# Local and global attention with a gated feed-forward: global rows of batches 4 to 7 loaded, cast and transposed later, and the last q and k of batch 1 ahead of the last w_in columns

## The chip, the core and the metric

The kernel runs on one core of one Trainium2 chip. The metric is the device time of one execution in microseconds (us). A core has TensorE (PE, matmuls; PEld is its weight load), VectorE (DVE), ScalarE (ACT), GpSimd (POOL) and SyncE (SP); here SP issues nearly all DMAs, and POOL a few. Each engine takes its instructions in the order of its own queue and waits on semaphores for others.

## The reference

Eight batches, eight heads, 512 local and 32 global rows of width 64. A global row attends to all 544 rows, a local row to the 32 global ones and to the local ones within 32 places. Then the heads are put side by side (512 columns) and go through a feed-forward with 2048 hidden columns.

```python
k_all = np.concatenate([k_g, k_l], axis=2); v_all = np.concatenate([v_g, v_l], axis=2)
out_g = np.matmul(sm(scale * np.matmul(q_g, k_all.transpose(0, 1, 3, 2))), v_all)
mask = np.abs(pos[:, None] - pos[None, :]) <= 32
s_ll = np.where(mask, scale * np.matmul(q_l, k_l.transpose(0, 1, 3, 2)), -1e9)
s_lg = scale * np.matmul(q_l, k_g.transpose(0, 1, 3, 2))
out_l = np.matmul(sm(np.concatenate([s_lg, s_ll], axis=-1)), v_all)
x = np.concatenate([out_g, out_l], axis=2).transpose(0, 2, 1, 3).reshape(-1, 512)
h = x @ w_in
out = (h * np.clip(h + 3.0, 0.0, 6.0) / 6.0) @ w_out
```

## The kernel before

**Pairs and batches.** The unit of attention is a pair of heads: pair p is batch b = p // 4 with m = p % 4, so there are 32 pairs. Pairs 0 to 7 (batches 0 and 1) stand in a sequence written out by hand; pairs 8 to 31 run in one loop (L760). Between the parts of a pair, `M(n)` puts n units of the feed-forward of an earlier batch. A unit of the first kind (`u1`, L421) makes 128 hidden columns from `win`: 4 matmuls into `psH`, then ACT (L426) and DVE (L428) make `gt`. One of the second kind (`u2`, L437) adds 4 matmuls to an output tile `po`. PSUM tiles come from one pool of 7 banks.

**One pair.** `load(p)` (L121, L124): SP loads k, q and v into three of 16 staging tiles `stg`. `cast(p)` (L137): POOL makes fp16 of them; `vshift` (L141) copies v once more, shifted by half a block, into `vb`. For pairs 0 to 7 `emit_T(p)` (L223) transposes k and q on TensorE; later pairs use DMA transposes issued by SP, `emit_TD(p)` (L244 for kT, L245 for qT), and a short POOL copy, `wrap_q(p)` (L251). `emit_S2(p)` (L263) makes the scores in two halves of 8 matmuls, each ending in ACT's exponential (L267) and a mask on DVE (L270). In tile `kT`, which holds all four pairs of a batch, each block is 128 local columns and 32 global ones; the first half of the scores reads local columns alone, the second also the global ones. `emit_SG(p)` (L306) scores the global rows; `emit_AV(p)` (L332, L335) and `emit_PG(p)` multiply by v; `emit_X(p)` sends the result `xn` back by a DMA transpose of SP (L388), or, for batches 0 and 1 and pair 11, by TensorE (L393).

**Global rows.** k_g and q_g come in three steps: `load_g(b0, b1, name)` (SP, L180), `cast_G` (POOL or DVE, L188), `emit_G` (4 TensorE transposes into `psGT`, L198, then 4 DVE copies into `kgT` or `qgz`, L206). For batches 4 to 7 each name is one load, one cast and one `emit_G`. `kglob(b)` (POOL, L210) copies kgT of batch b into the global columns of that batch's kT tile; kT tiles alternate between two.

**Order.** Within the loop everything for SP and POOL is put in the program's order by `pin`. At the top of pair p stands `feed(p)` (L708), with work for later pairs: `wrap_q(p + 2)`; at m = 0 two POOL copies of the next batch's v_g (L144, L149); `cast(p + 4)` and `vshift(p + 4)`; `kglob(b + 1)` at m = 1; then on SP `emit_TD(p + 3)` and `load(p + 5)`. After it come the scores of pair p + 1, `emit_SG(p + 1)`, `emit_AV(p)`, `emit_PG(p)` and `emit_X(p)`, with units between. The global rows of batches 4 to 7 are loaded at p = 9, cast on POOL at p = 11 and transposed at p = 12.

**The beginning.** The loads stand in one list. Each load of w_in (L160) is 512 columns of one of four row blocks, so that columns 1536 to 2047, units 12 to 15, need loads 12 to 15. POOL casts (L171) most of them in the same order as they are loaded.

Of the kernel before, what the change touches and what calls it, by code (L numbers as in the profile page):

```python
# [14 lines left out]
def kernel(  # L15
# [12 lines left out]
    nc = tc.nc  # L28
    P = 128
    B, H, Sl, D = q_l.shape  # L30
# [3 lines left out]
    NM = H // 2  # L34
# [20 lines left out]
    def ps_tile(name, dtype=FP32):  # L55
        return psp.tile([P, 2048 // (4 if dtype == FP32 else 2)], dtype, tag="ps", name=name)
# [54 lines left out]
    def stage():  # L111
        return wrk.tile([P, 512], FP32, tag="stg", name="stg", bufs=NSTG)

    def load(p, what="kqv"):
        b, m = divmod(p, NM)
        s = st.setdefault(p, {})
        for c in what:
            src = {"k": k_l, "q": q_l, "v": v_l}[c]
            t = stage()
            if c != "v" and b < NRUN:  # L120
                nc.sync.dma_start(out=t.rearrange("p (h x) -> p h x", h=2),  # L121
                                  in_=src[b, 2 * m:2 * m + 2].rearrange("h (p j) d -> p h (j d)", j=NT))
            else:
                nc.sync.dma_start(out=t.rearrange("p (h kb d) -> p (h kb) d", h=2, kb=NT),  # L124
                                  in_=src[b, 2 * m:2 * m + 2].rearrange("h (kb p) d -> p (h kb) d", p=P))
            s[c + "f"] = t.rearrange("p (h kb d) -> p kb h d", h=2, kb=NT)

    def cast(p, what, eng):
        b, m = divmod(p, NM)
        s = st[p]  # L130
        for c in what:
            if c == "v":
                o = vts[b % NV][:, :, m, vc].rearrange("p kb (h d) -> p kb h d", h=2)
            else:
                s[c + "n"] = wrk.tile([P, NT, P], FP16, tag=c + "n", name=c + "n", bufs=4)
                o = s[c + "n"].rearrange("p kb (h d) -> p kb h d", h=2)
            eng.tensor_copy(out=o, in_=s[c + "f"])  # L137

    def vshift(p, eng):
        b, m = divmod(p, NM)  # L140
        eng.tensor_copy(out=vbs[b % NV][0:D, :, m, vc], in_=vts[b % NV][D:P, :, m, vc])  # L141

    def vglob(b, eng):
        eng.tensor_copy(out=vbs[b % NV][rg, :, :, vc],  # L144
                        in_=vg[rg, b].rearrange("s (m h) d -> s m (h d)", h=2).unsqueeze(1)
                        .to_broadcast([Sg, NT, NM, P]))

    def vgsum(b, eng):
        eng.tensor_copy(out=vgs[b % NV][rg], in_=vg[rg, b])  # L149

    def load_vg(b):
        nc.gpsimd.dma_start(out=vg[rg, b], in_=v_g[b].rearrange("h s d -> s h d"))
# [3 lines left out]
    def load_w(kind, i):  # L156
        t = stage()
        if kind == "in":
            qd, m = divmod(i, NM)
            nc.sync.dma_start(out=t, in_=moe_w_in[m * P:(m + 1) * P, qd * 512:(qd + 1) * 512])  # L160
        else:
            nc.sync.dma_start(out=t, in_=moe_w_out[i * P:(i + 1) * P, :])
        w_st[kind, i] = t

    def cast_w(kind, i, eng):
        if kind == "in":
            qd, m = divmod(i, NM)
            o = w_in_t[m][:, qd * 512:(qd + 1) * 512]
        else:
            o = w_out_t[i // 4][:, i % 4]  # L170
        (eng.copy if eng is nc.scalar else eng.tensor_copy)(out=o, in_=w_st[kind, i])  # L171
# [5 lines left out]
    def load_g(b0, b1, nm):  # L177
        src = {"kg": k_g, "qg": q_g}[nm]
        t = stage()
        nc.sync.dma_start(  # L180
            out=t[:, 0:(b1 - b0) * HH * D].rearrange("p (n d) -> p n d", d=D),
            in_=src[b0:b1].rearrange("b (x y) s d -> (y s) (b x) d", x=HH))
        gst[b0, nm] = t

    def cast_G(b0, b1, nm, eng=nc.vector):
        n = wrk.tile([P, 4 * P], FP16, tag="gn", name=nm + "n", bufs=2)
        nb = b1 - b0
        eng.tensor_copy(out=n[:, 0:nb * P], in_=gst[b0, nm][:, 0:nb * P])  # L188
        gst[b0, nm, "n"] = n

    def emit_G(b0, b1, nm):
        nb = b1 - b0
        if (b0, nm, "n") not in gst:
            cast_G(b0, b1, nm)
        n = gst[b0, nm, "n"]
        psT = ps_tile("psGT", FP16)
        for j in range(nb):
            nc.tensor.matmul(out=psT[:, j * P:(j + 1) * P], lhsT=n[:, j * P:(j + 1) * P],  # L198
                             rhs=ident, is_transpose=True)
        MH = NM // HH  # L200
        for x in range(HH):
            kv = psT[x * D:(x + 1) * D, 0:nb * P].rearrange("p (b m e s) -> p e b m s", b=nb, m=MH, e=2)
            for e in range(2):
                r, ms = slice(e * D, (e + 1) * D), slice(x * MH, (x + 1) * MH)
                o = kgT[r, ms, b0:b1] if nm == "kg" else qgz[r, ms, b0:b1, e]
                nc.vector.tensor_copy(out=o.rearrange("p m b s -> p b m s"), in_=kv[:, e])  # L206

    def kglob(b, eng):
        kv = kTs[b % 2][:, :, 0:NT * KW].rearrange("p m (u c) -> p m u c", u=NT)
        eng.tensor_copy(out=kv[:, :, :, P:KW],  # L210
                        in_=kgT[:, :, b].unsqueeze(2).to_broadcast([P, NM, NT, Sg]))
# [37 lines left out]
    def wrap_q(p):  # L249
        qT = st[p]["qT"]  # L250
        nc.gpsimd.tensor_copy(out=qT[:, 0:W], in_=qT[:, Sl:Sl + W])  # L251
# [130 lines left out]
    def emit_X(p):  # L382
        b, m = divmod(p, NM)
        xn = st[p]["xn"]
        if b > NRUN or (b == NRUN and m < NM - 1):
            xt = wrk.tile([P, Sl], FP16, tag=f"xt{m}", name=f"xt{m}", bufs=2)
            xts.setdefault(b, []).append(xt)
            nc.sync.dma_start_transpose(out=xt.rearrange("p (w c) -> p w c", w=NT),  # L388
                                        in_=xn.rearrange("p w c -> p (w c)"))
            return  # L390
        psX = ps_tile("psX", FP16)
        for w in range(NT):
            nc.tensor.matmul(out=psX[:, w * P:(w + 1) * P], lhsT=xn[:, w], rhs=ident,  # L393
                             is_transpose=True)
        xt = wrk.tile([P, Sl], FP16, tag=f"xt{m}", name=f"xt{m}", bufs=2)
        xts.setdefault(b, []).append(xt)
        nc.vector.tensor_copy(out=xt, in_=psX[:, 0:Sl])  # L397
# [68 lines left out]
    def M(n):  # L466
        for _ in range(n):
            if units:
                units.pop(0)()
# [26 lines left out]
    load(6, "kq")  # L496
    load(4, "v")
    load(5, "v")
    for i in range(12, NC):
        load_w("in", i)  # L500
    load(7, "kq")
    load(6, "v")
    load(7, "v")
    load_g(0, 4, "qg")
# [58 lines left out]
    def first(p, what="kqv"):  # L563
        cast(p, what, nc.gpsimd)
        vshift(p, nc.gpsimd)
# [15 lines left out]
    cast(6, "kq", nc.gpsimd)  # L581
    first(4, "v")
    first(5, "v")
    for i in range(12, NC):
        cast_w("in", i, nc.gpsimd)
    cast(7, "kq", nc.gpsimd)
    first(6, "v")
    first(7, "v")
    vgsum(0, nc.gpsimd)
# [118 lines left out]
    def feed(p):  # L708
        b, m = divmod(p, NM)
        if 2 * NM <= p + 2 < NPAIR:  # L710
            wrap_q(p + 2)
        if p + 4 < NPAIR:
            if m == 0:
                vglob(b + 1, nc.gpsimd)
                vgsum(b + 1, nc.gpsimd)
            cast(p + 4, "kqv", nc.gpsimd)
            vshift(p + 4, nc.gpsimd)
        if m == 1 and b + 1 < B:
            kglob(b + 1, nc.gpsimd)
        if m == 2 and b + 2 < B:  # L720
            load_vg(b + 2)
        if 2 * NM <= p + 3 < NPAIR:
            emit_TD(p + 3)
        if p + 5 < NPAIR:
            load(p + 5)
# [34 lines left out]
    for p in range(2 * NM, NPAIR):  # L760
        b, m = divmod(p, NM)
        feed(p)
        if p == 9:
            load_g(4, B, "kg")
            load_g(4, B, "qg")
        if p == 11:
            cast_G(4, B, "kg", nc.gpsimd)
            cast_G(4, B, "qg", nc.gpsimd)
        if p == 12:
            emit_G(4, B, "kg")  # L770
            emit_G(4, B, "qg")
        n = (1, 1, 1, 2) if p == 2 * NM else (1, 1, 2, 2) if b == 2 else (1, 2, 2, 3)
        M(n[0])
        if m == 0 and b > NRUN:
            emit_den(b - 1)
            emit_XG(b - 1)
        if p + 1 < NPAIR:
            emit_S2(p + 1)
        M(n[1])
        if p + 1 < NPAIR:  # L780
            emit_SG(p + 1)
        M(n[2])
        emit_AV(p)
        emit_PG(p)
        M(n[3])
        emit_X(p)
        if m == NM - 1:
            units += moe_units(lambda mm, b=b: xts[b][mm], Sl, local_dests(b), last=(b == B - 1))
        pin(*QUEUES)
# [41 lines left out]
```

## Time and profile before

| | |
|---|---|
| Median of 13 runs | 328.85 us (327.89 to 330.01) |
| The profiled execution | 329.3 us |
| Its span, first to last instruction | 327.5 us |
| Mean granted TensorE clock | 0.979 |
| DMA | 53.57 MB, mean 164 GB/s |

The page cuts the span into 40 slices of 8.19 us; a digit is the busy share in tenths:

```profile
PE   7898789999994899999999999999999999999995
...
DVE  6758639799662669747974697469755882379201
ACT  6758736888450369636973697369736970479100
POOL 4866697598873865474567445845331110000000
...
DMA  8999989999999997988878998978744003100132
```

And the chain of work that ended last, by engine:

```profile
PE 81%; DMA 7%; DVE 3%; SPq 3%; POOL 2%; ACT 2%; issue 1%; POOLq 0%
```

In the busy rows, a low digit of PE is a stretch in which TensorE waited, or in which little was to be done (the start and the end). In a timeline each row is start, length, engine, line, operation and tiles; brackets give the idle time of the engine before it and what ended that. "SPq" rows are SP's issuing of DMAs. All times are from the span's start.

### The profile page before, as it was taken

What the parts mean: (1) busy time and instruction counts of PE and PEld (TensorE: products, weight loads), DVE (VectorE), ACT (ScalarE), POOL (GpSimd) and SP (SyncE); (2) the same over time, 40 slices, a digit from 0 to 9 for tenths busy, and PEclk for the clock granted to TensorE, in tenths of its full rate; (3) what the DMA queues carried; (4) which work ended last, traced back from release to release, by engine and by line L of the source; (5) the groups of instructions that cost most, each with busy time, mean ns of one, the idle gap of its engine ahead of it and who ended that gap; (6) DMA issues with size and microseconds to landing.
All of it is one profiled execution on the core that took longest, in us unless ns stands there. A gap on an engine that the chain in (4) does not pass through costs nothing.

```text
span 327.5 us, 7295 instructions
## 1 busy us (share of the span) xinstructions
PE 309.2 (94%) x2657; PEld 162.8 (50%) x2657; DVE 212.8 (65%) x480; ACT 198.3 (61%) x396; POOL 157.0 (48%) x295
## 2 busy tenths in 40 slices
PE   7898789999994899999999999999999999999995
PEld 4454346554552455555555555555555554448444
DVE  6758639799662669747974697469755882379201
ACT  6758736888450369636973697369736970479100
POOL 4866697598873865474567445845331110000000
PEclk9999959999999599999999999999999999999999
DMA  8999989999999997988878998978744003100132
GB/s 205 250 286 321 242 237 330 233 183 219 189 218 203 187 213 146 148 193 202 164 147 197 212 148 151 206 197 151 142 118 110 16 16 92 70 0 2 32 90 73
DMA packets 142436, 53.57 MB, mean 164 GB/s; under 512 B 129728, under 2 KB 134080, under 8 KB 142400
## 3 DMA queue, kind: packets, MB, share of 16 engines
q1 hardware_dynamic: 140224, 52.84, 70.9%
q0 software_dynamic: 2176, 0.26, 2.0%
q8 instruction: 21, 0.34, 0.5%
q14 instruction: 15, 0.12, 0.2%
HBM read 35.13 MB, written 8.91 MB: 134 GB/s over the span
## 4 chain that ended last, share of the span: by engine, by line
PE 81%; DMA 7%; DVE 3%; SPq 3%; POOL 2%; ACT 2%; issue 1%; POOLq 0%
PE po L437 35%; PE psH L421 32%; PE psS L263 4%; DMA stg<-in_v_l_dram 3%; DMA stg<-in_moe_w_in_dram 2%; DMA stg<-in_q_l_dram 2%; PE pav L332 2%; PE pav L335 2%; DVE gt L428 2%; SPq L121 2%; PE psSG L306 1%; PE pg L372 1%; PE po L449 1%; PE psS L276 1%; ACT t L426 1%
## 5 line engine op out<-in xcount | busy, mean ns | idle before, releaser
L437 PE MATMUL po<-wout,gt 128*128 128x512 f16 x528 | 124.2, 383 | 0.0
L421 PE MATMUL psH<-xt,win 128*128 128x512 f16 x512 | 120.4, 381 | 0.5 <-DVE xt L397 0.5
L428 DVE SCALAR_TENSOR_TENSOR gt<-t,psH 128x512 f16<-128x512 f32 (+1 forms) x144 | 90.9, 652 | 30.4 <-ACT t L426 29.1
L426 ACT ACTIVATE t<-psH,half_col 128x512 f32<-128x512 f32 (+1 forms) x144 | 92.0, 669 | 16.7 <-PE psH L421 15.5
L421 PEld LDWEIGHTS <-win 128*128 128x128 f16 x576 | 53.3, 98 | 52.4 <-issue 1.2
L437 PEld LDWEIGHTS <-gt 128*128 128x128 f16 x528 | 48.9, 99 | 53.4 <-issue 1.0
L267 ACT ACTIVATE E<-psS 128x512 f16<-128x512 f32 x96 | 49.4, 604 | 17.2 <-PE psS L263 17.1
L270 DVE TENSOR_TENSOR E<-E,mk 128x512 f16<-128x512 f16 x96 | 50.8, 565 | 11.6 <-ACT E L267 10.5
L441 ACT COPY ot<-po 128x512 f32<-128x512 f32 x16 | 9.4, 587 | 45.7 <-PE po L437 45.2
L137 POOL CAST kn<-stg 128x512 f16<-128x512 f32 x31 | 19.3, 623 | 27.4 <-DMA stg<-in_k_l_dram 27.0
L358 POOL TENSOR_TENSOR s<-Eg 128x128 f32<-128x128 f16 x24 | 11.3, 471 | 43.2 <-ACT Eg L307 42.9
L340 DVE TENSOR_TENSOR xn<-pav,rc 128x256 f16<-128x256 f32 x64 | 26.1, 422 | 1.4
L441 DVE COPY ot<-po 128x512 f32<-128x512 f32 x17 | 11.7, 689 | 21.1 <-PE po L437 17.4
L137 POOL CAST qn<-stg 128x512 f16<-128x512 f32 x31 | 19.3, 621 | 12.8 <-DMA stg<-in_q_l_dram 12.2
L137 POOL CAST vt<-stg 128x512 f16<-128x512 f32 x32 | 20.1, 627 | 8.6 <-DMA stg<-in_v_l_dram 7.8
L141 POOL COPY vb<-vt 64x512 f16<-64x512 f16 x32 | 20.5, 639 | 2.1
L292 ACT ACTIVATE E<-psS 128x512 f16<-128x512 f32 x32 | 17.3, 598 | 5.2 <-PE psS L288 4.9
L332 PE MATMUL pav<-vt,E 128*128 128x65 f16 x256 | 20.4, 195 | 0.0
L335 PE MATMUL pav<-vb,E 128*128 128x65 f16 x256 | 20.4, 196 | 0.0
L332 PEld LDWEIGHTS <-E 128*128 128x128 f16 x256 | 18.2, 100 | 3.5 <-issue 0.2
L335 PEld LDWEIGHTS <-E 128*128 128x128 f16 x256 | 17.2, 98 | 3.0
L405 ACT ACTIVATE Lg<-pg 64x128 f32<-64x128 f32 x16 | 4.3, 269 | 22.5 <-PE pg L379 22.4
(93 smaller groups left out, 284.3 us busy)
## 6 DMA issues: line engine op xcount, KB each, us to landing
stg<-in_k_l_dram SPq DMA_DIRECT2D x32, 256.0 KB, 3.5
stg<-in_q_l_dram SPq DMA_DIRECT2D x32, 256.0 KB, 4.4
stg<-in_v_l_dram SPq DMA_DIRECT2D x32, 256.0 KB, 4.8
out_dram<-ot SPq DMA_DIRECT2D x23, 256.0 KB, 3.3
stg<-in_moe_w_in_dram SPq DMA_DIRECT2D x16, 256.0 KB, 6.1
stg<-in_moe_w_out_dram SPq DMA_DIRECT2D x16, 256.0 KB, 4.7
out_dram<-ot SPq DMA_DIRECT2D x8, 192.0 KB, 3.9
out_dram<-ot SPq DMA_DIRECT2D x16, 64.0 KB, 1.9
```

The costliest lines, as they stand in the source:

```text
L137: eng.tensor_copy(out=o, in_=s[c + "f"])
L141: eng.tensor_copy(out=vbs[b % NV][0:D, :, m, vc], in_=vts[b % NV][D:P, :, m, vc])
L267: nc.scalar.activation(out=E[:, ch, e], in_=pss[2 * ch + e], func=EXP, scale=qk_scale)
L270: nc.vector.tensor_tensor(out=E[:, ch, e], in0=E[:, ch, e], in1=mk[:, ch].rearrange("p w c -> p (w c)"), op=mult)
L332: nc.tensor.matmul(out=o, lhsT=E[:, 0, e, w * P:(w + 1) * P], rhs=vt[:, w, m, c], start=True, stop=False, skip_group_check=True)
L335: nc.tensor.matmul(out=o, lhsT=E[:, 1, e, w * P:(w + 1) * P], rhs=vb[:, (w - 1) % NT, m, c], start=False, stop=True, skip_group_check=True)
L340: nc.vector.tensor_tensor(out=xn[:, 2 * w2:2 * w2 + 2].rearrange("p w (e d) -> p w e d", e=2), in0=po[:, :, 1:1 + P].rearrange("p w (e d) ...
L421: nc.tensor.matmul(out=ps[:, 0:n], lhsT=w_in_t[m][:, c * P:(c + 1) * P], rhs=rhs(m), start=(m == 0), stop=(m == NM - 1), skip_group_check= ...
L426: nc.scalar.activation(out=t1[:, 0:n], in_=ps[:, 0:n], func=RELU, bias=half_col, scale=1.0 / 6.0)
L428: nc.vector.scalar_tensor_tensor(out=gts[c][:, 0:n], in0=t1[:, 0:n], scalar=1.0, in1=ps[:, 0:n], op0=amin, op1=mult)
L437: nc.tensor.matmul(out=po[t][:, 0:dm], lhsT=gts[c][:, t * P:(t + 1) * P], rhs=w_out_t[c // 4][:, c % 4], start=(c == 0), stop=(c == NC - 1))
L441: (nc.scalar.copy if t % 2 else nc.vector.tensor_copy)(out=ot, in_=po[t][:, 0:dm])
```

## The change

Three edits. The load and the cast of k and q of pair 7 stand ahead of loads and casts 12 to 15 of w_in. The global rows of batches 4 to 7 are loaded at p = 10 instead of 9, cast at p = 12 instead of 11, and transposed at p = 14 instead of 12, the q rows at the end of that pair, ahead of `emit_X`. And `kglob(4)`, which reads what the transpose of the k rows makes, moves from pair 13 (m = 1) to pair 15 (m = 3), in both cases behind the casts in `feed`; the other batches keep m = 1. No instruction is added or taken away.

```diff
@@ -496,9 +496,9 @@
     load(6, "kq")
     load(4, "v")
     load(5, "v")
+    load(7, "kq")
     for i in range(12, NC):
         load_w("in", i)
-    load(7, "kq")
     load(6, "v")
     load(7, "v")
     load_g(0, 4, "qg")
@@ -581,9 +581,9 @@
     cast(6, "kq", nc.gpsimd)
     first(4, "v")
     first(5, "v")
+    cast(7, "kq", nc.gpsimd)
     for i in range(12, NC):
         cast_w("in", i, nc.gpsimd)
-    cast(7, "kq", nc.gpsimd)
     first(6, "v")
     first(7, "v")
     vgsum(0, nc.gpsimd)
@@ -715,7 +715,7 @@
                 vgsum(b + 1, nc.gpsimd)
             cast(p + 4, "kqv", nc.gpsimd)
             vshift(p + 4, nc.gpsimd)
-        if m == 1 and b + 1 < B:
+        if m == (NM - 1 if b == 3 else 1) and b + 1 < B:
             kglob(b + 1, nc.gpsimd)
         if m == 2 and b + 2 < B:
             load_vg(b + 2)
@@ -760,15 +760,14 @@
     for p in range(2 * NM, NPAIR):
         b, m = divmod(p, NM)
         feed(p)
-        if p == 9:
+        if p == 10:
             load_g(4, B, "kg")
             load_g(4, B, "qg")
-        if p == 11:
+        if p == 12:
             cast_G(4, B, "kg", nc.gpsimd)
             cast_G(4, B, "qg", nc.gpsimd)
-        if p == 12:
+        if p == 14:
             emit_G(4, B, "kg")
-            emit_G(4, B, "qg")
         n = (1, 1, 1, 2) if p == 2 * NM else (1, 1, 2, 2) if b == 2 else (1, 2, 2, 3)
         M(n[0])
         if m == 0 and b > NRUN:
@@ -783,6 +782,8 @@
         emit_AV(p)
         emit_PG(p)
         M(n[3])
+        if p == 14:
+            emit_G(4, B, "qg")
         emit_X(p)
         if m == NM - 1:
             units += moe_units(lambda mm, b=b: xts[b][mm], Sl, local_dests(b), last=(b == B - 1))
```

## The prediction
> **What bounds the kernel now.** I read the page first, then TensorE's own waits, then the chain of waits around the longest of them, and last the timelines of TensorE, POOL and SP between 84 and 139 us.
>
> ```profile
> PE 309.2 (94%) x2657; PEld 162.8 (50%) x2657; DVE 212.8 (65%) x480; ACT 198.3 (61%) x396; POOL 157.0 (48%) x295
> PEclk9999959999999599999999999999999999999999
> ```
>
> TensorE is busy for 94% of the span, so only its idle stretches and its slow stretches can be won. The second row shows two slices (each 8.19 us) at half clock: the sixth and the fourteenth. TensorE's waits name what precedes them (total, times, longest):
>
> ```profile
> PE psGT L198 <- POOL kgn L188: 6.3, 1, 6.3
> PE psTk L223 <- POOL kn L137: 3.1, 2, 2.2
> ```
>
> The windows (PE busy, PEld, DVE, ACT, POOL, clock, DMA share, GB/s) price both:
>
> ```profile
> 41.40:48.20 6.80, 6.37 (x46) 3.14 (x48) 2.11 (x6) 2.44 (x5) 6.11 (x12) 0.50 0.81 225
> 101.60:106.20 4.60, 0.01 (x1) 0.00 (x0) 0.26 (x1) 0.00 (x0) 1.74 (x4) 1.00 1.02 266
> 106.20:113.10 6.90, 5.18 (x33) 2.71 (x34) 3.94 (x12) 2.55 (x7) 5.98 (x11) 0.51 0.81 166
> ```
>
> The late stall is 6.31 us idle and then 5.2 us of work (107.9 to 113.1) at half clock, which loses 2.6: 8.9 us. The early one is 2.25 + 0.22 us idle and 6.6 us of work at half clock, 3.3 lost: 5.8 us. The diff aims at both. The chain (start, length) tells why the late one lasts: not the global rows are late, but what stands before their cast on POOL.
>
> ```profile
> 101.46 4.39 DMA stg<-in_v_l_dram
> ...
> 107.25 0.62 POOL kgn L188
> 107.88 0.05 issue
> 107.92 0.61 PE psGT L198 x4
> ```
>
> POOL works in order: `cast_G` stands behind `cast(15)`, whose v was issued by SP only at 101.46. So I asked what SP does. In SP's timeline from 84 us, every row starts within 0.15 us of the end of the one before, up to here:
>
> ```profile
> 124.07 0.77 SPq L124 DMA_DIRECT2D stg<-in_v_l_dram  x1
> 127.25 1.22 SPq L388 DMA_TRANSPOSE xt<-xn  x1
> 128.57 1.20 SPq L244 DMA_TRANSPOSE kT<-kn  x1
> 129.87 1.97 SPq L245 DMA_TRANSPOSE qT<-qn  x1
> 131.90 0.57 SPq L124 DMA_DIRECT2D stg<-in_k_l_dram  x1
> 132.53 0.57 SPq L124 DMA_DIRECT2D stg<-in_q_l_dram  x1
> 133.14 1.06 SPq L124 DMA_DIRECT2D stg<-in_v_l_dram  x1
> ```
>
> The gap of 2.41 us before 127.25 is SP's first wait for compute (for xn of pair 13). Until then its queue is a train without gaps, which TensorE neither hurries nor delays. The loads at 131.90 to 133.14 are those of pair 19.
>
> [...]
>
> **Part 1: k and q of pair 7 ahead of w_in 12 to 15.** Two loads and two casts pass four; nothing is added. The k cast takes the place of the first w_in cast on POOL (36.52 instead of 40.94), so pair 7's transposes no longer wait at 39.4. The last w_in cast ends about 1.5 us later (near 42.3 instead of 40.76), and the unit that needs it, at 45.25 now, would come near 41.2: it waits about 1 us. At that point some 4.5 us are gained. What is late next: the scores of pair 9 (75.62) need a POOL copy that ends at 73.81 + 0.46 = 74.3 behind a gapless POOL, so at most 1.3 us passes; those of pair 14 need a POOL copy that ends at 110.3, behind SP. By itself this part is worth 0 to 1.3 us at pair 9, and less behind what follows.
>
> **Part 2: the global rows later.** The two loads (1.01 + 1.14 us of SP) move from behind pair 14's loads to behind pair 15's. Both places lie ahead of pair 19's loads, so the train is as long as before. The two POOL casts (2 x 0.61) move behind `feed(12)`, ready near 117; the 8 transposes (2 x 0.43 at half clock) and 8 DVE copies (1.20 + 1.19) move to pair 14. TensorE no longer stops at 101.6. It then runs ahead, held only by pair 14's copy at 110.3, and reaches the scores of pair 16 at 110.3 + 2 x 8.35 (128.32 to 136.67 is one pair) = 127, plus about 0.5 for the transposes: 127.5. The DVE copies come while DVE is busy (7.45 of 9 us from 128 to 137). I cost them at nothing, since the wait below covers them; uncovered they cost at most 2.4.
>
> **Part 3: `kglob(4)` later.** This is the step that decides. kgT for batch 4 is now written only at pair 14, so the POOL copy into kT moves from `feed(13)` to the end of `feed(15)`, and its reader, the second half of `emit_S2(16)`, is issued just after. The slack before was wide (121.91 + 0.69 = 122.6 against 136.95):
>
> ```profile
> 121.91 0.69 POOL L210 COPY kT<-kgT 128x512 f16<-128x512 f16 x1
> ...
> 137.61 0.62 POOL L137 CAST vt<-stg 128x512 f16<-128x512 f32 x1 [0.26 <-DMA stg<-in_v_l_dram]
> 138.29 0.68 POOL L141 COPY vb<-vt 64x512 f16<-64x512 f16 x1
> ```
>
> ```profile
> 136.67 0.62 PE L263 MATMUL psS<-qT,kT 64*128 64x128 f16 x16
> ```
>
> In the changed program's instruction order `kglob(4)` follows the last of these rows (the casts of pair 19). Before, they end at 138.97, already 2 us after TensorE needs the copy. The SP train gives back only its gap: 2.41 - 0.09 = 2.3 us. Pair 19's v is then issued at 130.8, lands 4.5 (as before) to 5.0 us later (as pair 18's: 124.07 to 129.05), so its cast starts at 135.3 to 135.8; cast 0.68 and shift 0.74 with gaps, then 0.69: `kglob(4)` ends at 137.4 to 137.9. The first 8 score matmuls do not read the global columns; the second half started at 136.67 + 0.28 = 136.95. So TensorE is 0.45 to 1.0 us later at the same instruction; I take 0.7. It has stood still for about 10 us (127.5 to 137.6): whatever was gained before is spent here, by both parts.
>
> After it the clock is halved. [...] the two stalls of this trace cost 3.3 and 2.6. I take 2.6. From 137 to 268 us the chain is TensorE's, so nothing later absorbs it.
>
> Sum at the end: -8.9 and -5.8 removed, all given back by the wait, +0.7 (0.45 to 1.0), +2.6 (1.7 to 3.4) = +3.3 us (2.1 to 4.4). The profiled execution took 329.3 us (span 327.5, 1.8 around it): 332.6. It lies 0.45 above the median of 328.85, so 332.2 against the median.
>
> **Rivals.**
> - *The SP train shrinks (faster).* One place: the stretched rows between 84 and 134, such as 2.04 and 1.98 instead of 1.22 for xt, 1.97 instead of 1.20 for qT. Stretch in all: 0.82 + 0.76 + 0.77, 0.59 + 0.49 + 0.28 for three loads, about 1.0 for the global rows: 4.7 us. [...] `kglob(4)` ends at 132.9 and the result is 0.7 - 4.7 + 2.6 = -1.4: 327.4. It decides once `kglob(4)` ends before 136.95 - 2.6 = 134.3. If the wait vanished wholly, it would be -8.9, 319.9. For it: DMA share falls to 0.81 in 106 to 113. Against: nothing that the change moves relieves the DMA queue. 10%.
> - *The loads land later (slower still).* SP now issues without its gap, so pair 19's rows follow pair 18's closely; two of the stretches above once more, and landing at 6 us, make 2 us more: 334.2. DMA share of 0.98 and 1.09 in 110 to 126 speaks for it. 13%.
> - *No half clock after the wait.* +0.7 alone: 329.5. Against: both stalls here were followed by it, one of only 2.25 us. 5%.
> - *The change does not do what it says.* The orders of POOL, SP and TensorE show all moves as written; only the early part's effect at the end can be nil, which my sum already has.
>
> **How the numbers follow.** Forecast 72% (330.9 to 333.3), the rivals 10, 13 and 5%. The range leaves out the faster rival and the top of the slower one: 329.5 to 334.8. About 0.2% (0.66 us) can be told from no change. Slower: 72 + 13 and a part of the 5%, 0.86; no change 0.04; faster 0.10.
>
> **What would show it.** Right: no wait before psGT near 101 us, a TensorE idle of 8 to 11 us inside or just before `emit_S2(16)` ended by POOL's kT copy (L210), a half-clock slice after it, and none at 106 to 113; pair 7's transposes without their wait; SP without a gap near 125. Wrong: `kglob(4)` done before TensorE arrives, or a span under 326 us.

## The result and the profile after

| | before | after |
|---|---|---|
| Median | 328.51 us (325.43 to 330.5, 48 runs) | 331.51 us (329.66 to 333.22, 11 runs) |
| The profiled execution | 329.3 us | 330.81 us |
| Its span | 327.5 us | 329.0 us |
| Mean granted TensorE clock | 0.979 | 0.983 |

The changed kernel is slower: the ratio is 1.0099, with a 95% interval of 1.0073 to 1.0125, or about 3 us. The prediction said 3.3 us.

From the page of the changed kernel: the busy row, the clock in 40 slices of the span (8.2 us each), and the chain that ended last, by engine.

```profile
PE 308.0 (94%) x2657; PEld 161.6 (49%) x2657; DVE 209.8 (64%) x480; ACT 198.1 (60%) x396; POOL 155.4 (47%) x295
PEclk9999999999999799699999999999999999999999
PE 60%; DMA 21%; POOL 8%; SPq 6%; DVE 2%; issue 2%; ACT 1%; POOLq 0%
```

There are again two slices with a low clock, but the sixth is back at full speed, and it is now the 14th and the 17th. DMA's share of the chain rose from 7% to 21%, TensorE's fell from 81% to 60%: more of the way to the end now runs over transfers. TensorE's waits in the changed kernel (total, times, longest):

```profile
PE psS L263 <- POOL kT L210: 6.3, 1, 6.3
PE psH L421 <- DMA xt<-xn: 2.7, 1, 2.7
PE po L437 <- POOL wout L171: 1.7, 5, 0.4
PE psS L263 <- POOL qT L251: 1.6, 1, 1.6
```

Before, the list began with `psGT` waiting 6.3 us for `kgn` and `psTk` waiting 3.1 us for `kn`. The first is gone; of the second 0.2 us are left, at an earlier pair, and pair 7's transposes wait no more. In their place stands a wait of the same length for `kglob(4)` (L210), and a new one of 2.7 us that the prediction did not have: the feed-forward waits for the transposed x of pair 10. TensorE's timeline shows where the first lies:

```profile
130.03 0.40 PE L263 MATMUL psS<-qT,kT 64*128 64x128 f16 x8
136.74 0.61 PE L263 MATMUL psS<-qT,kT 64*128 64x128 f16 x8 [6.31 <-POOL kT L210]
```

The 16 matmuls of the scores of pair 16, one row before the change, are cut in two: the first eight run at 130.03, the second eight, which read the global columns, 6.31 us after the first are through. The chain of waits of the changed kernel names what they waited for:

```profile
127.48 1.21 SPq L245
...
129.98 4.68 DMA stg<-in_v_l_dram
...
134.72 0.61 POOL vt L137
...
135.39 0.62 POOL vb L141
136.01 0.05 issue
136.06 0.62 POOL kT L210
136.69 0.04 issue
136.74 0.61 PE psS L263 x8
```

This is the chain of before with pair 19 in the place of pair 15: a v load issued late by SP, its cast and its shift on POOL, then a step for the global rows that is itself long ready (DVE's last copy into kgT ends at 122.8), and TensorE. Only the last step has changed, from the cast of k_g to the copy of the global k columns. The chain names the load that came last, but q of pair 19 is nearly as late, as POOL's timeline shows:

```profile
134.00 0.61 POOL L137 CAST qn<-stg 128x512 f16<-128x512 f32 x1 [1.01 <-DMA stg<-in_q_l_dram]
134.72 0.61 POOL L137 CAST vt<-stg 128x512 f16<-128x512 f32 x1
```

By these rows an earlier v alone would have won less than 0.2 us (an estimate: 134.72 less the end of the cast before it); it is the three loads of pair 19 together that hold the queue. SP's timeline in the changed kernel:

```profile
122.69 1.11 SPq L124 DMA_DIRECT2D stg<-in_v_l_dram  x1
124.25 1.22 SPq L388 DMA_TRANSPOSE xt<-xn  x1
...
129.98 1.08 SPq L124 DMA_DIRECT2D stg<-in_v_l_dram  x1
```

The gap of 2.41 us in SP's queue is down to 0.45, and pair 19's v is issued at 129.98 instead of 133.14. The windows (start and end, length, then PE, PEld, DVE, ACT and POOL busy, clock, DMA share, GB/s) price the two waits:

```profile
106.02:108.71 2.69, 0.01 (x1) 0.00 (x0) 0.00 (x0) 0.20 (x1) 0.00 (x0) 1.00 1.35 95
109.51:112.92 3.41, 3.41 (x20) 1.36 (x19) 1.38 (x2) 1.70 (x3) 2.62 (x3) 0.50 1.30 229
130.43:136.74 6.31, 0.01 (x2) 0.01 (x2) 0.90 (x3) 1.08 (x2) 4.07 (x9) 0.74 1.07 185
136.74:140.23 3.49, 3.49 (x15) 1.37 (x16) 1.03 (x3) 1.09 (x2) 0.00 (x0) 0.50 1.10 220
```

Each wait is followed by work at half clock (0.50 in the windows), 3.41 and 3.49 us of it. Half of that is lost, by an estimate from TensorE's timeline: eight matmuls of L437 took 3.34 us from 137.28, of which 2.95 lie at half clock, and 1.89 us from 140.60, with the clock back at 1.00 (2.95 / 2 + 0.39 = 1.87). The last row matters most: the second half of the scores of pair 16 starts 0.21 us earlier than before (136.74 against 136.95), and 1.75 us are lost after it. That is +1.5, and the two profiled executions differ by 330.81 - 329.3 = 1.51 us.

### The profile page after: what moved, and what is told of

Same layout as the page of the kernel before. It is cut to its first block, busy times and chain, and to the rows that moved or that the text cites. A ratio compares the mean times of both kernels' runs of the same rounds, so it can differ in the third digit from the quotient of the medians.

```text
span 329.0 us, 7297 instructions
## 1 busy us (share of the span) xinstructions
PE 308.0 (94%) x2657; PEld 161.6 (49%) x2657; DVE 209.8 (64%) x480; ACT 198.1 (60%) x396; POOL 155.4 (47%) x295
## 4 chain that ended last, share of the span: by engine, by line
PE 60%; DMA 21%; POOL 8%; SPq 6%; DVE 2%; issue 2%; ACT 1%; POOLq 0%
PE po L437 26%; PE psH L421 25%; DMA stg<-in_v_l_dram 9%; DMA stg<-in_moe_w_out_dram 5%; DMA stg<-in_moe_w_in_dram 4%; SPq L124 3%; PE psS L263 3%; POOL vt L137 2%; SPq L121 1%; POOL vb L141 1%; DVE gt L428 1%; DMA stg<-in_q_l_dram 1%; PE pav L335 1%; PE pav L332 1%; DMA qT<-qn 1%
## 5 line engine op out<-in xcount | busy, mean ns | idle before, releaser
L437 PE MATMUL po<-wout,gt 128*128 128x512 f16 x528 | 124.7, 383 | 1.7 <-POOL wout L171 1.7
L421 PE MATMUL psH<-xt,win 128*128 128x512 f16 x512 | 121.8, 383 | 3.9 <-DMA xt<-xn 2.7
L437 PEld LDWEIGHTS <-gt 128*128 128x128 f16 x528 | 48.8, 98 | 55.0 <-issue 3.6
L270 DVE TENSOR_TENSOR E<-E,mk 128x512 f16<-128x512 f16 x96 | 48.1, 540 | 12.1 <-ACT E L267 11.1
L137 POOL CAST qn<-stg 128x512 f16<-128x512 f32 x31 | 19.5, 629 | 10.6 <-DMA stg<-in_q_l_dram 10.2
L263 PE MATMUL psS<-qT,kT 64*128 64x128 f16 x384 | 15.6, 222 | 7.9 <-POOL kT L210 6.3
L263 PEld LDWEIGHTS <-kT 64*128 64x128 f16 x384 | 11.2, 96 | 18.1 <-issue 10.4
L332 PEld LDWEIGHTS <-E 128*128 128x128 f16 x256 | 17.8, 99 | 3.4
```

What stands on the lines that cost most here:

```text
L263: nc.tensor.matmul(out=pss[2 * ch + e][:, w * P:(w + 1) * P], lhsT=kT[r, c0:c0 + P], rhs=qT[r, w * P:(w + 1) * P])
L270: nc.vector.tensor_tensor(out=E[:, ch, e], in0=E[:, ch, e], in1=mk[:, ch].rearrange("p w c -> p (w c)"), op=mult)
L332: nc.tensor.matmul(out=o, lhsT=E[:, 0, e, w * P:(w + 1) * P], rhs=vt[:, w, m, c], start=True, stop=False, skip_group_check=True)
L421: nc.tensor.matmul(out=ps[:, 0:n], lhsT=w_in_t[m][:, c * P:(c + 1) * P], rhs=rhs(m), start=(m == 0), stop=(m == NM - 1), skip_group_check= ...
L437: nc.tensor.matmul(out=po[t][:, 0:dm], lhsT=gts[c][:, t * P:(t + 1) * P], rhs=w_out_t[c // 4][:, c % 4], start=(c == 0), stop=(c == NC - 1))
```

## The experiments

My theory is that of the prediction: GpSimd's queue puts `kglob(4)` behind pair 19's v, TensorE stops there, and whatever the other parts of the change gain is spent in that wait. The rivals are that the later rows themselves cost the time, that the early part counts with its whole stall, and that the transfers bound this stretch wherever the copy stands.

| Kernel | median, us | before beside it | ratio, 95% interval |
|---|---|---|---|
| early_only | 328.57 | 328.78 | 0.9994 (0.9971 to 1.0017) |
| rows_only | 332.71 | 328.78 | 1.0100 (1.0070 to 1.0129) |
| kglob_late_alone | 333.08 | 328.78 | 1.0121 (1.0094 to 1.0148) |
| kglob_at_14 | 321.66 | 328.78 | 0.9782 (0.9751 to 0.9814) |
| kglob_15_front | 326.43 | 328.96 | 0.9940 (0.9908 to 0.9972) |
| load19_first | 331.74 | 328.96 | 1.0101 (1.0050 to 1.0152) |
| kglob_at_14_no_early | 323.76 | 328.96 | 0.9856 (0.9818 to 0.9894) |
| kglob_at_14_rows_11 | 323.64 | 328.96 | 0.9852 (0.9804 to 0.9899) |
| load19_wrap_last | 329.63 | 328.84 | 1.0018 (0.9997 to 1.0040) |
| kglob_at_14_again | 322.30 | 328.84 | 0.9821 (0.9778 to 0.9863) |
| kglob_at_14_no_early_again | 323.04 | 328.84 | 0.9820 (0.9785 to 0.9855) |

Kernels with the same time of before beside them ran on one chip.

### The early part alone

The kernel before, with k and q of pair 7 moved as in the change:

```diff
     load(5, "v")
+    load(7, "kq")
     for i in range(12, NC):
         load_w("in", i)
-    load(7, "kq")
...
+    cast(7, "kq", nc.gpsimd)
     for i in range(12, NC):
         cast_w("in", i, nc.gpsimd)
-    cast(7, "kq", nc.gpsimd)
```

> The kernel before with the early part of the change alone: last q and k of the second batch (pair 7) ahead of the w_in columns 12 to 15; the global rows stay where they were. My theory: the early stall shrinks, but what TensorE gains there it gives back at the next waits for GpSimd and for the transfers (qT of pair 9 by about 74, pair 14 at about 110, the v load of pair 19), so the end moves by -0.3 to +0.3 us, at most -1.3. Rival, that the early stall was worth its length: its 2.25 us and the half clock after it, 4 to 5 us faster.

The ratio's interval includes 1 (no change) and excludes the rival's 4 us. TensorE's waits in this kernel show where the gain went:

```profile
PE psGT L198 <- POOL kgn L188: 8.4, 1, 8.4
PE psS L263 <- POOL qT L251: 1.8, 1, 1.8
```

The wait for `kgn` is 8.43 us long instead of 6.31. TensorE comes to it earlier and stands there longer, and the wait for `qT` of pair 9 takes 1.8 us on the way. In this execution (327.33 us, 1.2 under the median) the stop still ends 1.24 us earlier than before, at 106.68, and less work falls into the half clock after it (3.4 us instead of 5.2), so that 2.0 us of the gain are left; in the medians 0.2 us are.

### The later rows without the early part

> The changed kernel without the early part (pair 7's q and k stay behind the w_in columns). My theory: the same wait for GpSimd's last kT copy at the scores of pair 16 ends at the same time, about 136.7, so the time is that of the changed kernel within 0.5 us, about 3 us over before. Rival, that the two parts add up (the early part a gain of 4 us inside the change): about 4 us slower than the changed kernel, 7 us over before. Other rival, that the early part causes the loss: 0 over before.

The edit is that of the early part, reversed, in the changed kernel. The ratio is 1.0100 against 1.0099 of the change: the early part neither causes the loss nor helps against it. The longest wait of TensorE here:

```profile
PE psS L263 <- POOL kT L210: 8.1, 1, 8.1
```

It ends at 137.22, 0.5 us after that of the changed kernel. TensorE reached the scores at 128.75 here, 1.3 us earlier than in the changed kernel, and waits 1.8 us longer.

### The late copy alone

The kernel before, with its rows as early as they were, and one line of the change:

```diff
-        if m == 1 and b + 1 < B:
+        if m == (NM - 1 if b == 3 else 1) and b + 1 < B:
             kglob(b + 1, nc.gpsimd)
```

> The kernel before with one step moved: the copies of the global k columns of the third batch (kglob(4)) go into the last feed, where the change has them, while the global rows are loaded, cast and transposed as early as before. My theory: GpSimd's kT copy ends about 0.6 to 0.7 us after vb of pair 19, near 139.7 where the kernel before has its old stall end at 136.95, so TensorE waits about 2.7 us more and the kernel is 2.7 to 4.5 us slower. Rival, that where these copies stand does not matter and only the later load and cast cost: 0.

4.3 us slower. POOL's timeline in this kernel, where kgT had been ready for long:

```profile
137.05 0.62 POOL L137 CAST vt<-stg 128x512 f16<-128x512 f32 x1 [0.33 <-DMA stg<-in_v_l_dram]
137.73 0.68 POOL L141 COPY vb<-vt 64x512 f16<-64x512 f16 x1
138.47 0.69 POOL L210 COPY kT<-kgT 128x512 f16<-128x512 f16 x1
```

TensorE's timeline beside it:

```profile
139.22 0.40 PE L263 MATMUL psS<-qT,kT 64*128 64x128 f16 x8 [2.71 <-POOL kT L210]
```

Data that has been ready since 108.9 (DVE's last copy into kgT) is copied at 138.47, because GpSimd takes it behind a load. This one line, without any later row, costs no less than the whole change.

### The copy ahead of the feed of pair 14

The changed kernel, with transposes and copy at the top of pair 14:

```diff
         b, m = divmod(p, NM)
+        if p == 14:
+            emit_G(4, B, "kg")
+            kglob(4, nc.gpsimd)
         feed(p)
...
-        if p == 14:
-            emit_G(4, B, "kg")
...
-        if m == (NM - 1 if b == 3 else 1) and b + 1 < B:
+        if m == 1 and b != 3 and b + 1 < B:
```

> The changed kernel with the global k columns of the third batch (their transposes and the copies) at the top of pair 14's iteration, ahead of its feed, so that GpSimd reaches them at about 122, before it waits for the v load of pair 19; all else as in the change. My theory: no wait for the kT copy at the scores of pair 16, TensorE goes through there at 130.0 instead of 136.7 and keeps its full clock: 6.7 plus about 1.75 us, some 8 us faster than the changed kernel, about 323, faster than both. Rival, that the transfers bound this stretch anyway and the next wait takes the place of this one: 329 or more.

321.66 us, about 2% faster than before and 3% faster than the changed kernel; more than expected. POOL's timeline:

```profile
122.15 0.81 POOL L210 COPY kT<-kgT 128x512 f16<-128x512 f16 x1
124.11 0.21 POOL L251 COPY qT<-qT 128x32 f16<-128x32 f16 x1 [1.15 <-DMA qT<-qn]
```

TensorE's timeline there, where the 16 matmuls are one row again:

```profile
128.11 0.62 PE L263 MATMUL psS<-qT,kT 64*128 64x128 f16 x16
```

And its page's row of the granted clock:

```profile
PEclk9999999999999999999999999999999999999999
```

No wait at these scores, and no slice at half clock; a wait of 1.70 us for the transposed x near 107 is left. The transfers do not bound this stretch; the rival falls.

### The copy at the front of the last feed

Half the dose: in the changed kernel the copy stands at the front of `feed(15)`, ahead of `wrap_q(17)` and of the casts of pair 19.

```diff
     def feed(p):
         b, m = divmod(p, NM)
+        if p == 15:
+            kglob(4, nc.gpsimd)
...
-        if m == (NM - 1 if b == 3 else 1) and b + 1 < B:
+        if m == 1 and b != 3 and b + 1 < B:
```

> The changed kernel with the copies of the global k columns (kglob(4)) at the front of the last feed, ahead of wrap_q(17) and the transposes of q and k of pair 17, instead of behind the casts of pair 19's v. My theory, that only the place of these copies in GpSimd's queue counts: GpSimd reaches them at about 131.2 to 131.9, so TensorE, which is there at 130.0, waits 1.2 to 2 us instead of 6.3: 4.5 to 6 us faster than the changed kernel, between it and the kernel with the copies at pair 14. Rival, that what cost the time is the later load, cast and transpose of the rows: no gain over the changed kernel.

326.43 us lies between the two, as expected. POOL's timeline:

```profile
131.79 0.61 POOL L210 COPY kT<-kgT 128x512 f16<-128x512 f16 x1
132.34 0.21 POOL L251 COPY qT<-qT 128x32 f16<-128x32 f16 x1
```

The second half of the scores starts at 132.46, at once after the copy. The wait before it is 4.35 us, not 1.2 to 2, because TensorE reached it at 127.71 here.

### Pair 19's load earlier on SP

The changed kernel, with one swap at p = 14 (the loads of k, q and v of pair 19 all move):

```diff
+        if p == 14:
+            load(p + 5)
         if 2 * NM <= p + 3 < NPAIR:
             emit_TD(p + 3)
-        if p + 5 < NPAIR:
+        if p != 14 and p + 5 < NPAIR:
             load(p + 5)
```

> The changed kernel with the load of pair 19's v issued ahead of the transposes of q and k of pair 17 on SyncE's queue; GpSimd's order is untouched, the kT copy still stands behind the casts of that v. My theory, that the wait of TensorE is the wait of GpSimd for this transfer: it lands and the copies end about 3 us earlier (133.7 instead of 136.7), about 3 us faster than the changed kernel. Rival, that the place on SyncE's queue does not matter (the transfers are bound by what they share): 0.

My theory fell here: 331.74 us, the ratio of the change. SP's timeline in this kernel:

```profile
127.84 0.58 SPq L124 DMA_DIRECT2D stg<-in_v_l_dram  x1
128.52 1.97 SPq L244 DMA_TRANSPOSE kT<-kn  x1
130.60 1.20 SPq L245 DMA_TRANSPOSE qT<-qn  x1
```

POOL's timeline:

```profile
133.87 0.21 POOL L251 COPY qT<-qT 128x32 f16<-128x32 f16 x1 [2.46 <-DMA qT<-qn]
...
136.48 0.61 POOL L210 COPY kT<-kgT 128x512 f16<-128x512 f16 x1
```

The load is issued 2.1 us earlier (127.84 against 129.98), but pair 17's qT transpose 3.1 us later (130.60 against 127.48), and `wrap_q(17)`, which waits for that transpose, stands ahead of the casts in GpSimd's queue. GpSimd now waits 2.46 us there instead, and the casts that follow find their data landed. In this timeline nothing passes the copy that waits: the next cast, which has no wait of its own, starts at 134.02, after the 2.46 us. I had traced only one of the two transfers that stand ahead of the copy.

### The same, with the short copy behind

To tell that from a load that lands later when asked for earlier, `wrap_q(17)` goes behind `kglob(4)` as well:

```diff
-        if 2 * NM <= p + 2 < NPAIR:
+        if 2 * NM <= p + 2 < NPAIR and p != 15:
             wrap_q(p + 2)
...
             kglob(b + 1, nc.gpsimd)
+        if p == 15:
+            wrap_q(p + 2)
```

> The kernel with pair 19's load ahead of pair 17's transposes on SyncE, and in addition GpSimd's short copy of pair 17's qT (wrap_q(17)) moved behind the casts of pair 19 and the kT copy, so that GpSimd's queue no longer meets the transpose before the loads. My theory after the last kernel, that GpSimd waits for the last of both transfers, in the order of its own queue: the casts of pair 19 start near 131.4, the v of pair 19 (issued near 127.8) lands by 132.5, the kT copy ends at 134.0 to 134.6 instead of 137.1, and the kernel is 2 to 3 us faster than the one with the load alone moved (about 329 against 331.7). Rival, that the load only lands later when it is asked for earlier (the transfers share one rate): the copy ends at 136.5 or later, 0.

329.63 us, 2.1 less than with the load alone moved; the intervals of the two ratios do not meet. POOL's timeline:

```profile
131.56 0.62 POOL L137 CAST vt<-stg 128x512 f16<-128x512 f32 x1
132.24 0.61 POOL L141 COPY vb<-vt 64x512 f16<-64x512 f16 x1
132.92 0.62 POOL L210 COPY kT<-kgT 128x512 f16<-128x512 f16 x1
133.47 0.21 POOL L251 COPY qT<-qT 128x32 f16<-128x32 f16 x1
```

No bracket: GpSimd waits for neither transfer, and the copy ends at 133.54 instead of 137.09. The load did land earlier: v is cast at 131.56, where in the changed kernel it landed at 134.66. So the copy had been held by the later of two transfers, in the order of GpSimd's queue. With both out of the way, what stands before it is GpSimd's own work, without a gap back to v of pair 18, which landed at 127.35.

### One account for all

From the second half of the scores of pair 16 on, TensorE has no wait of note in any of these kernels, so the end should move by the start of that instruction plus what half clock takes after it. The loss is taken as half of the stretch at clock 0.50 in the windows, the estimate above; where a window holds both clocks, the share follows from its mean (0.57 over 4.85 us after the wait of load19_first: 4.17 us at half clock, 2.1 lost). The last two columns are against before.

| Kernel | second half starts, us | lost at half clock after it | sum | profiled executions |
|---|---|---|---|---|
| before | 136.95 | 0 | 0 | 0 (329.3) |
| after | 136.74 | 1.75 | +1.5 | +1.5 |
| early_only | 134.59 + 0.28 | 0 | -2.1 | -2.0 |
| rows_only | 137.22 | 1.8 | +2.1 | +2.05 |
| kglob_late_alone | 139.22 | 1.7 | +4.0 | +4.1 |
| kglob_15_front | 132.46 | 2.8 | -1.7 | -1.8 |
| load19_first | 137.15 | 2.1 | +2.3 | +2.3 |
| load19_wrap_last | 133.59 | 3.0 | -0.4 | -0.4 |
| kglob_at_14 | 128.11 + 0.28 | 0 | -8.6 | -8.6 |

(0.28 is the distance of the second half from the first where nothing waits, as in the prediction.) Every row closes within about 0.1 us. Single executions lie up to 2.7 us from the median of their kernel (early_only's run from 326.02 to 329.49), and their mean granted clock differs too (0.979 to 0.994 in load19_wrap_last). By medians the order is the same but for two close pairs: kglob_15_front is faster than early_only, and load19_wrap_last just slower than before.

### What remains when the wait is gone

Two kernels ask what bounds the fastest one. The first leaves the early part out:

> The kernel with the copies of the global k columns at pair 14, without the early part (pair 7's q and k behind the w_in columns). My theory: with the wait for the kT copy gone, the early stall is no longer covered whole; it costs 0 to 2 us against the kernel with both, since TensorE still meets the wait for the transpose of x near 106. Rival, that the early part is worth its whole stall now: 4 to 5 us slower than the kernel with both. Other rival, that it is covered still: 0.

> The kernel with the copies of the global k columns at pair 14 once more, beside the one without the early part on the same chip, to price the early part where nothing covers it. My theory: about 321.7, 7 us under before; the early part is worth 1.5 to 2.5 us here, because TensorE still meets two waits it shares (qT near 74, the transpose of x near 106). Rival, that the 2 us seen between two chips is chance: the two agree within 0.7 us.

> The same without the early part (pair 7's q and k behind the w_in columns). My theory: about 323.8, 1.5 to 2.5 us slower than the kernel with it. Rival: equal within 0.7 us.

On two different chips the ratios with and without the early part were 0.9782 and 0.9856, with intervals that do not meet; on one chip 0.9821 and 0.9820, and medians 0.7 us apart. So the early part is worth something between nothing and 2 us once the cover is gone, and these runs do not settle it. The profiled executions lean to a gain: with it TensorE reaches the scores of pair 16 at 128.11 and 128.17, without it at 129.43 and 131.30; but these are two executions of each. That its whole stall of 5.8 us would count is excluded.

The second takes the loads of the global rows one pair later again, to pair 11, so that the transpose of x for pair 10 gets ahead of them:

> The kernel with the copies of the global k columns at pair 14, and the loads of the global rows one pair later again (at pair 11 instead of 10), behind the transpose of x for pair 10 on SyncE's queue. My theory: that transpose lands about 2 us earlier, the wait of the feed-forward for it (2.69 us near 106 in the changed kernel) shrinks or goes, 1 to 3 us faster than with the loads at pair 10. Rival, that the casts of the rows now come late and GpSimd or SyncE takes the gain back: 0, or slower.

No gain is seen; the median is 2 us over that of kglob_at_14 on another chip, and the two intervals overlap. The wait near 106 is gone, and TensorE reaches the scores of pair 16 at 127.60 instead of 128.11. But TensorE's timeline has this later on:

```profile
144.29 2.10 PE L421 MATMUL psH<-xt,win 128*128 128x512 f16 x9 [1.76 <-DMA xt<-xn]
```

The same kind of wait, one batch later: SP issues the transpose for it at 140.99, where kglob_at_14 issues it at 139.41. This wait accounts for the profiled execution (127.60 - 128.11 + 1.76 = +1.25 against kglob_at_14, measured 322.16 - 320.74 = +1.42). Why SP's queue is 1.6 us later there is not shown.

The version to keep is kglob_at_14: it beats both kernels in two sets of runs, at 321.66 and 322.30 us.

## Why the prediction was right

**Part 1** (0 to 1.3 us, less behind what follows): borne out. Pair 7's transposes no longer wait, the scores of pair 9 are held by POOL's qT until 73.82 (predicted 74.3, an end taken from before), and alone the part gives 0.9994. The wait of about 1 us for the last w_in cast measured 0.6 us in two pieces.

**Part 2**: the stop before `psGT` is gone, as said. That TensorE is held only by pair 14's copy was wrong. At 106 it waited 2.69 us for the transpose of x of pair 10; and 3.41 us at half clock followed. SP's timeline has this transpose here before and after, in both kernels behind the two loads of the global rows:

```profile
104.14 1.98 SPq L388 DMA_TRANSPOSE xt<-xn  x1
```

```profile
103.26 1.38 SPq L388 DMA_TRANSPOSE xt<-xn  x1
```

It is issued no later than before. What changed is TensorE: before, it began to read the x of this batch at 117.29, and now it stands ready for pair 10's at 106.02, while that lands only at 108.7. I followed pair 19's load across the moved loads, and for the transposes in between only asked whether the train becomes longer, not who waits for each. So TensorE reached the scores at 130.03, not 127.5, and waited 6.31 us, not about 10. In the four other kernels with both the rows and the copy late it came at 127.1 to 128.8: they wait there too, 1.9 to 2.4 us, but without half clock after it (1.00 in the windows up to 113). The end does not depend on it, because the wait that follows swallows it; in kglob_at_14 it does.

**Part 3**: the deciding step, and right in kind. Alone, it makes the old kernel 4.3 us slower; taken out of the change, it leaves 6 to 7 us of gain. Its size was off: I had `kglob(4)` end at 137.4 to 137.9, and it ended at 136.68. The transfer took 4.68 us, within the 4.5 to 5.0 assumed; the issue came 3.16 us earlier than before, where I had counted only the gap, at 2.3 us. The gap gave 1.96. SP's queue was 0.66 us ahead already at the transpose of x near 85 (85.25 instead of 85.91), and from there to the load its rows took 0.54 us less, a small piece of the rival that I gave 10%; that rival needed an end before 134.3. So the term of +0.7 measured -0.2. That SP only issues in its rows without gaps, and does not wait there, was my assumption; it was not shown.

**The half clock after it**: +2.6 taken, my estimate from the two stalls of before (3.3 and 2.6 lost), in a range of 1.7 to 3.4 whose ends that trace does not show; 1.75 in the profiled execution of the changed kernel, and 1.7 to 3.0 in the other kernels with this wait.

The sum for the profiled execution is thus +1.5 instead of +3.3, and the medians differ by +3.0: the profiled execution of before lies 0.8 us above its median, that of after 0.7 below. The forecast of 332.2 met the median of 331.51 more closely than its terms met one profile, in which both came out smaller; part of that is luck. Three of the signs I had named came otherwise: the idle time at the scores of pair 16 was 6.31 us and not 8 to 11, a half-clock stretch stood between 106 and 113 after all, and SP kept a gap of 0.45 us near 124. The rivals "loads later still" and "no half clock" did not occur.

## What to carry to other kernels

When a step on a strict queue is moved behind others, list every transfer that those others wait for; the step is ready when the last of them has landed, however old its own data is (in kglob_late_alone, data ready since 108.9 was copied at 138.47). A stall that is removed is worth only as far as the next thing whose time the stalled engine does not set: find that thing before adding up gains, and if it is a short copy, look for a place for it ahead of the waiting instruction. Here that place, fourteen GpSimd instructions earlier, turned 1% slower into 2% faster.

## What was not expected of the hardware

The length of a wait did not tell whether half clock followed it. Idle times of TensorE of 2.25 us (before, the early stall) and 2.69 us (after, near 106) were followed by it, while through and after one of 2.4 us (load19_wrap_last, at the same place) the clock stayed at 1.00. Apart from one at the end of each trace, the stretches at half clock were 6.83 us long twice in before (41.40 to 48.22 and 106.25 to 113.07), and 3.41 and 6.83 us in after (109.51 to 112.92 and 133.40 to 140.23). In load19_first one lasted about 10.2 us (131.0 to 141.3, an estimate from the mean clock of windows of 0.5 us). What starts such a stretch, and what sets its length, is not shown here.

What a wait cost was not told by its length either: the late copy's wait was followed by losses of 1.7 to 3.0 us, and a longer wait did not always lose more (6.31 us of waiting in after lost 1.75, 4.35 us in kglob_15_front lost 2.8). Half clock that passed within the wait cost nothing, as TensorE had no work there: it began 3.3 us before the end of the longer wait and 1.3 us before the end of the shorter, and lasted 6.83 us both times.
